# Sinkhorn attention and SwiGLU: a smaller mixing matrix, a reordered prologue, and two moved bursts

## The chip, the core and the metric

The program runs on one core of a Trainium2 chip. A core has engines that each run their own list of instructions in order and meet at semaphores: TensorE (PE in the profile; PEld is its weight load), VectorE (DVE), ScalarE (ACT), GpSimd (POOL) and SyncE (SP). TensorE multiplies a stationary operand (`lhsT`) by a moving one (`rhs`) into PSUM, of which this kernel uses eight banks of 512 floats a partition; VectorE and ScalarE read PSUM, and their copies out of it are called drains here. DMAs are issued from the queues of POOL, SP and ACT. The metric is the device time of one execution in microseconds, lower is better.

## The reference

Inputs are q, k, v of shape (4, 8, 768, 64), `sort_net` of shape (4, 8, 8, 8), and the weights of a SwiGLU block with a model width of 512 and an inner width of 1536. For each of 32 pairs of batch and head:

```python
P = sort_net
for _ in range(5):
    P = np.exp(P - np.max(P, axis=-1, keepdims=True))
    P = P / (np.sum(P, axis=-1, keepdims=True) + 1e-09)
    P = P / (np.sum(P, axis=-2, keepdims=True) + 1e-09)
k_sorted = np.einsum('bhij,bhjcd->bhicd', P, k_b)   # 8 blocks of 96 rows are mixed
v_sorted = np.einsum('bhij,bhjcd->bhicd', P, v_b)
attn = softmax(scale * q_b @ k_sb^T)                # within each block of 96
x = attn @ v_sb                                     # heads side by side: (3072, 512)
out = (silu(x @ w_gate) * (x @ w_val)) @ w_out
```

## The kernel before

**Sinkhorn (lines 218 to 241).** One 32x64 tile `p_ps` holds all matrices. Five rounds go back and forth between ScalarE (the exp) and VectorE (sums, reciprocals, products). The result is written to `p_bf`, repeated along a new axis of H = 8, in two operations of VectorE. TensorE has nothing to do yet: it runs small matmuls without use (`dots`, line 479) and 512-wide ones (`fill`, line 475), some of them tied to a round's `rowreds`.

**Mixing weights (lines 490 to 505).** `weights` transposes `p_bf` with the identity: eight matmuls for each half of the partitions write `w_ps`, where every one of 64 rows (head, block) holds the same matrix values that `mix_rows` on VectorE then masks to `rmix`, a block-diagonal matrix. With `rmix` as one operand a matmul mixes the blocks of k or v and transposes them at once.

**Chunks of batch 0 (lines 274 to 302, called in 506 to 517).** `q0_chunk`, `k0_chunk` and `v_chunk` each run some matmuls into a PSUM tile and drain it with VectorE ("v") or ScalarE ("s"). The last argument names the PSUM tile: "a" and "b" are two banks each, "x" is one, and "gen" rotates over three. A chunk has to wait until the tile's earlier reader is done. Queries come in two halves; `q0_chunk(0, 16, 8, "v", "a")` is the end of the first half.

**Attention units.** A unit is half of a batch's blocks for a pair of heads. `scores` runs its matmuls, `exps` the exps on ScalarE, `av` the value product on TensorE with a reciprocal and a product on VectorE (lines 362 to 366). The outcome is transposed into `xts`: on TensorE with a drain (`x_to`) for batch 0, and by a transposing DMA in SP's queue (`x_dma`) for the other batches. For batch 0's first four units the calls are written out by hand (lines 519 to 566); `early` starts the first gate and value tiles piece by piece, as the pieces of `xts[(0, 0)]` come.

**The feed-forward part.** It runs for eight half batches n: `gate(n, m)` and `value(n, m)` for twelve tiles m, each four matmuls of 384 columns, then `outp` for three output tiles of twelve matmuls. Gate tiles are read by a tanh on ScalarE, then by VectorE (line 420); value tiles by VectorE (line 433). All of them and some output tiles rotate through "gen".

**What sets the order.** On TensorE, ScalarE and POOL the order is that of the calls. `merge(main, side)` weaves the attention work of the next half batch into `ffn(n)`: each call of `ffn` has a cost (0.65 for a gate or value tile, 0.87 for a third of an output tile), and a side entry is called as soon as the sum of the costs has reached its time. `units` makes such entries: the scores of two units at `at`, the second unit's exp at `at + 1.3`, the two value products at `at + avs`. `v_pairs` makes entries for `v_pair_chunk`, the mixed values of batches 2 and 3, each with one drain of VectorE from "b" and one of ScalarE from "a"; `kqs` does the same for keys. VectorE's order is left to a scheduler after the prologue (line 569).

**Transfers.** POOL issues the loads in the order written. It copies batch 1's values (`copy_v`), then casts queries of batches 2 and 3 into a scratch (`q_cast`), then waits for batch 1's transposed output (`hold`, line 638) before it loads the next values. SP issues the transposing DMAs and the stores of the output.

Of the kernel before, what the change touches and what calls it, by code (L numbers as in the profile page):

```python
# [10 lines left out]
BF16 = mybir.dt.bfloat16  # L11
AF = mybir.ActivationFunctionType
ALU = mybir.AluOpType
# [4 lines left out]
def kernel(  # L18
# [191 lines left out]
    colred = const.tile([BH, 1, NB], FP32)  # L210
    p_bf = const.tile([BH, NB, H, NB], BF16)
    def pair_tile(name, tag):
        return psum.tile([128, 1024], FP32, name=name, tag=tag)

    def bank_tile(name, tag="gen"):
        return psum.tile([128, 512], FP32, name=name, tag=tag, bufs=3 if tag == "gen" else 1)

    p_ps = bank_tile("p_ps")[0:BH, 0:NB * NB].rearrange("p (i j) -> p i j", j=NB)
    for it in range(N_ITER):
# [15 lines left out]
        if it < N_ITER - 1:  # L235
            nc.vector.tensor_mul(p_ps, p_ps, colred.to_broadcast([BH, NB, NB]))
    for lo in (0, NB // 2):
        part = slice(lo, lo + NB // 2)
        nc.vector.tensor_tensor(
            p_bf[:, part], p_ps[:, part].unsqueeze(2).to_broadcast([BH, NB // 2, H, NB]),  # L240
            colred.unsqueeze(1).to_broadcast([BH, NB // 2, H, NB]), op=ALU.mult)
    copy_v(nc.scalar, 0, lowr, 4, 8)
    copy_v(nc.scalar, 0, lowr, 5, 8, 0, 40)

    def drain(eng, dst, src):
        if eng == "v":
            nc.vector.tensor_copy(dst, src)  # L247
        else:
            nc.scalar.copy(dst, src)  # L249
# [32 lines left out]

    def k0_chunk(at, n, eng, tag):
        dst = kqt_tile(0)[:, 0:GI * C].rearrange("p (n a c) -> p a n c", a=2, c=HC)
        rm = rmix[0].rearrange("p a (g two) i -> p two a g i", two=2)
        tp = chunk_tile("tk0", n // 8, tag).rearrange("p (l a n) -> p l a n", l=n, a=2)
        for lc in range(n):
            for two in range(2):
                nc.tensor.matmul(tp[two * D:(two + 1) * D, lc].rearrange("p a (g i) -> p a g i", g=H2),
                                 lhsT=k0[:, at + lc, :], rhs=rm[:, two], start=True, stop=True)  # L290
        drain(eng, dst[:, :, :, at:at + n], tp.rearrange("p l a n -> p a n l"))

# [25 lines left out]
    def scores(b, u, tag):  # L318
        half, g = divmod(u, H2)
        k_sb, k_at, q_sb, q_at = ((kqts[b], 0, kqts[b], GI * C) if b < 2 else  # L320
                                  (kqts["p"], (b - 2) * GI * C, kqts["q"], (b - 2) * GI * C))
        if tag == "gen":
            wide = None
            pss = [bank_tile("qk"), bank_tile("qk")]
        else:
            wide = pair_tile("qk", tag).rearrange("p (two n) -> p two n", two=2)
            pss = [wide[:, 0], wide[:, 1]]
        for i4 in range(4):
            at = (g * NB + half * 4 + i4) * C
            for two in range(2):  # L330
                lo = two * D
                nc.tensor.matmul(pss[two][:, i4 * C:(i4 + 1) * C],  # L332
                                 lhsT=k_sb[lo:lo + D, k_at + at:k_at + at + 128],
                                 rhs=q_sb[lo:lo + D, q_at + at:q_at + at + C],
                                 start=True, stop=True)
        return wide, pss
# [146 lines left out]

    dots(124)
    for it, n in ((1, 3), (2, 4), (3, 4), (4, 4)):
        nc.tensor.matmul(idle_ps[0:NB, 0:NB], lhsT=rowreds[it][:, :, 0], rhs=rowreds[it][:, :, 0],
                         start=True, stop=True)
        fill(idle_ps, n)

    w_ps = bank_tile("w_ps")[:, 0:NB * B * H].rearrange("p (i b h) -> p i b h", b=B, h=H)  # L490

    def weights(half):
        for i in range(NB):
            nc.tensor.matmul(w_ps[halves[half], i].rearrange("p b h -> p (b h)"),
                             lhsT=p_bf[:, i].rearrange("p a b -> p (a b)"),
                             rhs=ident[0:BH, 0:BH], start=True, stop=True)
# [4 lines left out]

    weights(0)
    weights(1)
    mix_rows(rmix[0][lowr, 0], lowr, 0)
# [7 lines left out]
    v_chunk(0, 56, 8, "s", "gen")  # L512
    k0_chunk(0, 16, "v", "a")
    k0_chunk(16, 16, "s", "b")
    k0_chunk(32, 8, "v", "gen")
    k0_chunk(40, 8, "s", "gen")
    q0_chunk(0, 16, 8, "v", "a")
    fill(idle_ps, 4)
    qk(0, 0, "a")
# [4 lines left out]
    qk(0, 2, "gen")  # L524
    idle_ps = bank_tile("idle_ps")
    fill(idle_ps, 2)
    av(0, 0, "a")
    fill(idle_ps, 2)
    av(0, 1, "b")
    fill(idle_ps, 1)  # L530
    xts[(0, 0)] = xtp.tile([128, H2, TW], BF16, name="xt0_0", tag="xt")
    qk(0, 3, "gen")
    av(0, 2, "a")
    x01 = xt_tile("x", 2)
    x_to(x01[:, 0], 0, 0)
    x_to(x01[:, 1], 0, 1)
    drain("s", xts[(0, 0)][:, 0:2, :], x01.rearrange("p g a b -> p g (a b)"))
    fill(idle_ps, 1)
    av(0, 3, "b")
    x2 = xt_tile("gen", 1)  # L540
    x_to(x2[:, 0], 0, 2)
    drain("s", xts[(0, 0)][:, 2:3, :], x2.rearrange("p g a b -> p g (a b)"))
    first = {}

    def early(n, kcs):
# [3 lines left out]
        for kc in kcs:  # L549
            nc.tensor.matmul(first[n], lhsT=sb[:, kc, ts(m, 128)], rhs=xts[(0, 0)][:, kc, :],  # L550
                             start=(kc == 0), stop=(kc == NKC - 1))

    early(0, (0, 1))
    early(1, (0, 1))
    x3 = xt_tile("x", 1)
    x_to(x3[:, 0], 0, 3)
    drain("v", xts[(0, 0)][:, 3:4, :], x3.rearrange("p g a b -> p g (a b)"))
    early(0, (2,))
    early(1, (2,))
    early(2, (0,))  # L560
    early(0, (3,))
    early(1, (3,))
    early(2, (1, 2, 3))
    gate_out(0, 0, first[0])
# [6 lines left out]

    def units(b, us, ats, avs=(1.9, 3.6), lag=3.1):
        us = list(us)
        todo = []
        for n, at in enumerate(ats):
            u, u2 = us[2 * n:2 * n + 2]
            held = []
            todo.append((at, lambda u=u, u2=u2, held=held: (qk(b, u, "b"), held.append(scores(b, u2, "a")))))
            todo.append((at + 1.3, lambda u2=u2, held=held: exps(b, u2, *held[0])))
            for w, tag, t in ((u, "b", avs[0]), (u2, "a", avs[1])):  # L580
                if b == 0:
                    todo.append((at + t, lambda w=w, tag=tag: av(b, w, tag)))
                    todo.append((at + t + lag, lambda w=w: drain("v", *xtr(b, w))))
                else:
                    todo.append((at + t, lambda w=w, tag=tag: (av(b, w, tag), x_dma(b, w))))
        return todo
# [44 lines left out]
    def q0_rest():  # L631
# [4 lines left out]
    merge(ffn(1), kqs(1, (0.6, 3.3, 7.1)) + vs(v_chunk, 16, (5.2, 5.8, 8.4, 9.1))  # L636
          + units(1, range(4), (11.0, 15.6), (1.3, 2.6)))
    hold = const.tile([1, 1], BF16)
# [3 lines left out]
    for s in range(4):  # L642
        copy_v(nc.gpsimd, 1, both, s)
    nc.vector.memset(kqt_tile("p")[:, 2 * GI * C:], 0.0)
    merge(ffn(2), units(1, range(4, 8), (0.0, 5.5)) + kqs("p", (13.0, 14.7, 20.7)) + v_pairs([(0, 22.5)])
          + [(13.0, lambda: q_dma(2)), (16.4, lambda: q_dma(3))])
    merge(ffn(3), v_pairs([(1, 0.0), (2, 5.1), (3, 6.9)]) + units(2, range(4), (9.8, 14.9)))
    merge(ffn(4), units(2, range(4, 8), (0.0, 8.0)))
# [38 lines left out]
```

## Time and profile before

| what | value |
|---|---|
| median of three runs | 246.46 us (246.25 to 246.61) |
| the profiled execution's own time | 246.0 us |
| its span | 244.2 us |
| TensorE matmuls busy | 237.1 us, 97% of the span, 2617 instructions |
| VectorE, ScalarE, POOL busy | 154.8, 112.3, 51.3 us |
| TensorE's granted clock, mean | 1.00 |
| batch 0's first scores start | 18.28 us |
| value tile (0, 1) starts | 25.27 us |

The page gives the busy time of each engine, the chain of work that ended last, and groups of instructions by line. A timeline row holds the start and the length of a group of equal instructions, its engine, line, operation, tiles (out<-in) and number; in brackets stands the idle time of the engine before it and what ended that. A matmul's length includes a tail in which the next one already runs: matmuls of 384 columns are 0.325 us long in the rows and 0.163 us apart. So a TensorE that looks busy can still have gaps, and starts are what counts. A wait shows as idle time with its releaser; a late transfer shows as a row whose releaser is a DMA.

### The profile page before, as it was taken

To read this page: it belongs to the slowest core of one execution; us is meant where nothing else is said; L and a number is where in the kernel's file an instruction comes from. 1 tells how busy PE (TensorE), PEld (TensorE's weight loads), DVE (VectorE), ACT (ScalarE), POOL (GpSimd) and SP (SyncE) were. 2 spreads that over 40 slices of the span, in tenths; PEclk is the share of its full clock that TensorE was granted. 3 is DMA by queue.
4 is the path that set the end of the run, shared out by engine and by line. 5 is a ranking of instruction groups with operands and counts; after the bars stand their busy time and mean duration, and the time that the engine had idled before them with its cause. 6 is when DMAs were issued, how large, how long until landed. Compare 5 with 4: busy or idle time off the path is not lost.

```text
span 244.2 us, 6162 instructions
## 1 busy us (share of the span) xinstructions
PE 237.1 (97%) x2617; PEld 139.4 (57%) x2617; DVE 154.8 (63%) x326; ACT 112.3 (46%) x189; POOL 51.3 (21%) x45
## 2 busy tenths in 40 slices
PE   7799999999999999999999999999999999999994
PEld 6375666676455565555555555565556555555543
DVE  6786789876664685777755845674675576445700
ACT  3977554467435435365543452254325334332312
POOL 5992139990002059200000000000000000000000
PEclk9999999999999999999999999999999999999999
DMA  5989999999996999410121212012111211110122
GB/s 99 215 129 208 206 213 213 204 214 190 161 137 139 190 162 159 119 43 3 46 75 32 62 59 71 8 59 63 32 43 46 75 36 43 43 43 3 43 86 86
DMA packets 39642, 24.77 MB, mean 101 GB/s; under 512 B 29376, under 2 KB 34368, under 8 KB 39616
## 3 DMA queue, kind: packets, MB, share of 16 engines
q0 software_dynamic: 19632, 14.16, 38.9%
q1 hardware_dynamic: 19840, 10.17, 17.0%
q8 instruction: 20, 0.33, 0.6%
q10 hardware_dynamic: 144, 0.07, 0.1%
q14 instruction: 6, 0.05, 0.1%
HBM read 28.32 MB, written 7.86 MB: 148 GB/s over the span
## 4 chain that ended last, share of the span: by engine, by line
PE 90%; DVE 4%; DMA 2%; ACT 1%; issue 1%; POOLq 0%
PE v_ps L428 25%; PE o_ps L445 25%; PE g_ps L410 25%; PE av_ps L359 3%; PE qk L332 3%; PE tkq L269 3%; DMA v<-in_v_dram 2%; PE o_ps L461 1%; PE idle_ps L477 1%; PE tv L300 1%; DVE st L365 1%; DVE vt L247 1%; PE tq L279 1%; PE tv L310 1%; PE g_ps L550 1%
## 5 line engine op out<-in xcount | busy, mean ns | idle before, releaser
L420 DVE SCALAR_TENSOR_TENSOR gs_sb<-th_sb,g_ps 128x384 bf16<-128x384 bf16 x96 | 52.9, 551 | 52.4 <-ACT th_sb L418 49.6
L428 PE MATMUL v_ps<-xt,wv_sb 128*128 128x384 bf16 x380 | 77.3, 326 | 0.0
L410 PE MATMUL g_ps<-xt,wg_sb 128*128 128x384 bf16 x376 | 76.6, 325 | 0.2
L418 ACT ACTIVATE th_sb<-g_ps 128x384 bf16<-128x384 f32 x96 | 47.1, 491 | 55.5 <-PE g_ps L410 52.7
L445 PE MATMUL o_ps<-wo,h 128*128 128x512 bf16 x276 | 64.2, 379 | 0.0
L433 DVE SCALAR_TENSOR_TENSOR h<-v_ps,gs_sb 128x384 bf16<-128x384 f32 x96 | 53.4, 556 | 7.6 <-PE tkq L269 0.5
L428 PEld LDWEIGHTS <-wv_sb 128*128 128x128 bf16 x380 | 35.3, 97 | 23.2 <-issue 0.2
L410 PEld LDWEIGHTS <-wg_sb 128*128 128x128 bf16 x376 | 34.9, 97 | 23.7 <-issue 0.4
L445 PEld LDWEIGHTS <-h 128*128 128x128 bf16 x276 | 26.1, 98 | 28.7
L450 ACT COPY o_sb<-o_ps 128x512 f32<-128x512 f32 x23 | 13.5, 586 | 49.0 <-PE o_ps L445 49.0
L148 POOL COPY vch<-v 64x1536 bf16<-64x1536 bf16 (+2 forms) x11 | 28.8, 2657 | 13.0 <-DMA v<-in_v_dram 12.9
L345 ACT ACTIVATE e_all<-qk 96x768 bf16<-96x768 f32 x30 | 23.3, 801 | 4.5 <-PE qk L332 4.5
L365 DVE TENSOR_TENSOR st<-av_ps,r_sb 96x512 bf16<-96x512 f32 x32 | 21.8, 680 | 0.3
L359 PEld LDWEIGHTS <-e_all 96*128 96x128 bf16 x256 | 11.8, 97 | 6.0 <-ACT e_all L345 1.7
L359 PE MATMUL av_ps<-vt,e_all 96*128 96x65 bf16 x256 | 13.1, 193 | 0.5 <-ACT e_all L345 0.5
L249 ACT CAST vt<-tv 96x1024 bf16<-96x1024 f32 (+1 forms) x11 | 10.1, 931 | 4.7 <-PE tv L310 3.6
L363 DVE RECIPROCAL r_sb<-av_ps 96x8 f32<-96x8 f32 x32 | 6.4, 199 | 8.7 <-PE av_ps L359 8.7
L247 DVE CAST vt<-tv 96x1024 bf16<-96x1024 f32 (+1 forms) x7 | 7.4, 1064 | 2.2 <-PE tv L310 1.7
L477 PE MATMUL idle_ps<-warm_sb 128*128 128x512 bf16 x25 | 7.6, 411 | 0.0
L247 DVE COPY oq_v<-o_ps 128x128 f32<-128x128 f32 x1 | 0.3, 292 | 9.3 <-PE o_ps L461 9.3
L395 POOL DMA_DIRECT2D q_scr<-in_q_dram x2 | 5.6, 3178 | 0.0
L146 ACT COPY vch<-v 64x768 bf16<-64x768 bf16 (+1 forms) x4 | 5.4, 1384 | 0.2 <-DMA v<-in_v_dram 0.2
(83 smaller groups left out, 129.8 us busy)
## 6 DMA issues: line engine op xcount, KB each, us to landing
out_dram<-o_sb SPq DMA_DIRECT2D x23, 256.0 KB, 2.0
v<-in_v_dram POOLq DMA_DIRECT2D x4, 384.0 KB, 12.6
wg_sb<-in_moe_w_gate_dram POOLq DMA_DIRECT2D x3, 512.0 KB, 11.2
wv_sb<-in_moe_w_val_dram POOLq DMA_DIRECT2D x3, 512.0 KB, 13.0
wo<-in_moe_w_out_dram POOLq DMA_DIRECT2D x3, 512.0 KB, 16.2
kqp<-in_k_dram POOLq DMA_DIRECT2D x2, 768.0 KB, 10.1
q_scr<-in_q_dram POOLq DMA_DIRECT2D x2, 768.0 KB, 18.8
v<-in_v_dram POOLq DMA_DIRECT2D x2, 768.0 KB, 9.8
```

Source lines behind the costliest of these rows:

```text
L148: eng.tensor_copy(dst, src.transpose([0, 2, 1]))
L247: nc.vector.tensor_copy(dst, src)
L345: nc.scalar.activation(e_all[:, n:n + 2, 0:4 * C], wide[0:C, :, 0:4 * C], AF.Exp, scale=scale)
L359: nc.tensor.matmul(o[:, two, i4, 0:D + 1], lhsT=e[:, i4 * C:i4 * C + 128], rhs=vt[:, 2 * g + two, half * 4 + i4, 0:D + 1], start=True, sto ...
L365: nc.vector.tensor_tensor(st.rearrange("p i two d -> p two i d"), o[0:C, :, :, 0:D], r_sb.to_broadcast([C, 2, 4, D]), op=ALU.mult)
L410: nc.tensor.matmul(g_ps, lhsT=wg_sb[:, kc, ts(m, 128)], rhs=xt[:, kc, :], start=(kc == 0), stop=(kc == NKC - 1))
L418: nc.scalar.activation(th_sb, g_ps, AF.Tanh, scale=0.5)
L420: nc.vector.scalar_tensor_tensor(gs_sb, th_sb, 1.0, g_ps, op0=ALU.add, op1=ALU.mult)
L428: nc.tensor.matmul(v_ps, lhsT=wv_sb[:, kc, ts(m, 128)], rhs=xt[:, kc, :], start=(kc == 0), stop=(kc == NKC - 1))
L433: nc.vector.scalar_tensor_tensor(h_tiles[n][:, m, :], v_ps, 0.5, gs_tiles.pop(m), op0=ALU.mult, op1=ALU.mult)
L445: nc.tensor.matmul(o_ps, lhsT=h_w[:, m, ts(t3, 128)], rhs=wo_sb[part][:, m % 4, :], start=(m == 0), stop=(m == NFC - 1))
L450: nc.scalar.copy(o_sb, o_ps)
```

## The change

These things are edited:

- `p_bf` is repeated 4 times instead of 8 and written by one operation; the mixing weights are then made by 32 matmuls of 32 rows each, four groups g for each block row i, instead of 16 of 64 rows.
- The useless matmuls are divided otherwise: 105 dots and 2 fillers instead of 124 dots at the start, one filler more in the last round, 3 fillers instead of 4 ahead of the first scores, one or two fewer between the first units.
- Batch 0's last query chunk runs ahead of the key chunks, in "x". The first key chunk is drained by ScalarE and the second by VectorE, the reverse of before. Of the two small key chunks ScalarE drains the first 16 of 32 columns each, and VectorE the rest.
- The fourth scores take one bank of "gen" and "x" ("mixed") instead of two of "gen"; the tile for the first two transposed pairs is in "gen" instead of "x" and drained in two copies.
- `early(0, (0, 1))` stands ahead of the third pair's transpose, and the pieces of the first three tiles follow in another order.
- `units` gets an argument `second`, which is 0.9 instead of 1.3 for batch 1's first four units.
- In `ffn(2)` the first value burst of batches 2 and 3 has the time 21.6 instead of 22.5, and the second is called there at 22.5 instead of at 0.0 in `ffn(3)`.

```diff
-    p_bf = const.tile([BH, NB, H, NB], BF16)
+    p_bf = const.tile([BH, NB, 4, NB], BF16)
...
-    for lo in (0, NB // 2):
-        part = slice(lo, lo + NB // 2)
-        nc.vector.tensor_tensor(
-            p_bf[:, part], p_ps[:, part].unsqueeze(2).to_broadcast([BH, NB // 2, H, NB]),
-            colred.unsqueeze(1).to_broadcast([BH, NB // 2, H, NB]), op=ALU.mult)
+    nc.vector.tensor_tensor(p_bf, p_ps.unsqueeze(2).to_broadcast([BH, NB, 4, NB]),
+                            colred.unsqueeze(1).to_broadcast([BH, NB, 4, NB]), op=ALU.mult)
...
-    def k0_chunk(at, n, eng, tag):
+    def k0_chunk(at, n, eng, tag, parts=None):
...
-        drain(eng, dst[:, :, :, at:at + n], tp.rearrange("p l a n -> p a n l"))
+        src = tp.rearrange("p l a n -> p a n l")
+        if parts is None:
+            drain(eng, dst[:, :, :, at:at + n], src)
+            return
+        drain(eng, dst[:, :, 0:parts, at:at + n], src[:, :, 0:parts])
+        return lambda e: drain(e, dst[:, :, parts:, at:at + n], src[:, :, parts:])
...
-        if tag == "gen":
+        if tag in ("gen", "mixed"):
             wide = None
-            pss = [bank_tile("qk"), bank_tile("qk")]
+            pss = [bank_tile("qk"), bank_tile("qk", "gen" if tag == "gen" else "x")]
...
-    dots(124)
-    for it, n in ((1, 3), (2, 4), (3, 4), (4, 4)):
+    dots(105)
+    fill(idle_ps, 2)
+    for it, n in ((1, 3), (2, 4), (3, 4), (4, 5)):
...
-    def weights(half):
-        for i in range(NB):
-            nc.tensor.matmul(w_ps[halves[half], i].rearrange("p b h -> p (b h)"),
+    for i in range(NB):
+        for g in range(4):
+            nc.tensor.matmul(w_ps[32 * g:32 * g + 32, i].rearrange("p b h -> p (b h)"),
                              lhsT=p_bf[:, i].rearrange("p a b -> p (a b)"),
                              rhs=ident[0:BH, 0:BH], start=True, stop=True)
...
-    k0_chunk(0, 16, "v", "a")
-    k0_chunk(16, 16, "s", "b")
-    k0_chunk(32, 8, "v", "gen")
-    k0_chunk(40, 8, "s", "gen")
-    q0_chunk(0, 16, 8, "v", "a")
-    fill(idle_ps, 4)
+    q0_chunk(0, 16, 8, "v", "x")
+    k0_chunk(0, 16, "s", "a")
+    k0_chunk(16, 16, "v", "b")
+    rest = [k0_chunk(at, 8, "s", "gen", 2 * NB) for at in (32, 40)]
+    for drain_rest in rest:
+        drain_rest("v")
+    idle_ps = bank_tile("idle_ps", "x")
+    fill(idle_ps, 3)
     qk(0, 0, "a")
     qk(0, 1, "b")
...
     qk(0, 2, "gen")
-    idle_ps = bank_tile("idle_ps")
-    fill(idle_ps, 2)
+    fill(idle_ps, 1)
     av(0, 0, "a")
     fill(idle_ps, 2)
     av(0, 1, "b")
-    fill(idle_ps, 1)
...
-    qk(0, 3, "gen")
+    qk(0, 3, "mixed")
     av(0, 2, "a")
-    x01 = xt_tile("x", 2)
+    x01 = xt_tile("gen", 2)
     x_to(x01[:, 0], 0, 0)
     x_to(x01[:, 1], 0, 1)
-    drain("s", xts[(0, 0)][:, 0:2, :], x01.rearrange("p g a b -> p g (a b)"))
-    fill(idle_ps, 1)
+    for g in range(2):
+        drain("s", xts[(0, 0)][:, g, :], x01[:, g].rearrange("p a b -> p (a b)"))
     av(0, 3, "b")
-    x2 = xt_tile("gen", 1)
-    x_to(x2[:, 0], 0, 2)
-    drain("s", xts[(0, 0)][:, 2:3, :], x2.rearrange("p g a b -> p g (a b)"))
...
+    x2 = xt_tile("gen", 1)
     early(0, (0, 1))
+    x_to(x2[:, 0], 0, 2)
+    drain("s", xts[(0, 0)][:, 2:3, :], x2.rearrange("p g a b -> p g (a b)"))
     early(1, (0, 1))
+    early(0, (2,))
     x3 = xt_tile("x", 1)
     x_to(x3[:, 0], 0, 3)
     drain("v", xts[(0, 0)][:, 3:4, :], x3.rearrange("p g a b -> p g (a b)"))
-    early(0, (2,))
     early(1, (2,))
-    early(2, (0,))
+    early(2, (0, 1, 2))
     early(0, (3,))
     early(1, (3,))
-    early(2, (1, 2, 3))
+    early(2, (3,))
...
-    def units(b, us, ats, avs=(1.9, 3.6), lag=3.1):
+    def units(b, us, ats, avs=(1.9, 3.6), lag=3.1, second=1.3):
...
-            todo.append((at + 1.3, lambda u2=u2, held=held: exps(b, u2, *held[0])))
+            todo.append((at + second, lambda u2=u2, held=held: exps(b, u2, *held[0])))
...
-          + units(1, range(4), (11.0, 15.6), (1.3, 2.6)))
+          + units(1, range(4), (11.0, 15.6), (1.3, 2.6), second=0.9))
...
-    merge(ffn(2), units(1, range(4, 8), (0.0, 5.5)) + kqs("p", (13.0, 14.7, 20.7)) + v_pairs([(0, 22.5)])
+    merge(ffn(2), units(1, range(4, 8), (0.0, 5.5)) + kqs("p", (13.0, 14.7, 20.7)) + v_pairs([(0, 21.6), (1, 22.5)])
           + [(13.0, lambda: q_dma(2)), (16.4, lambda: q_dma(3))])
-    merge(ffn(3), v_pairs([(1, 0.0), (2, 5.1), (3, 6.9)]) + units(2, range(4), (9.8, 14.9)))
+    merge(ffn(3), v_pairs([(2, 5.1), (3, 6.9)]) + units(2, range(4), (9.8, 14.9)))
```

More of the change, by code (lines that the diff above doesn't have):

```diff
@@ L500, in mix_rows @@
                                 w_ps[rows, :, b].transpose([0, 2, 1]), op=ALU.mult)
-    weights(0)
-    weights(1)
     mix_rows(rmix[0][lowr, 0], lowr, 0)
```

## The prediction

> **What bounds the kernel now.** I read the chain of waits first, then the timeline engine by engine for the stretches that the diff touches: the prologue up to 25.3 us, 60 to 65 us, 69 to 77 us and 100 to 109 us. All times are microseconds from the span's start.
>
> ```profile
> PE 90%; DVE 4%; DMA 2%; ACT 1%; issue 1%; POOLq 0%
> ```
>
> Nine tenths of the path are matmuls. From 25.27, where value tile (0,1) begins, TensorE works with small gaps to the end, so a delay or gain ahead of it shifts everything behind, unless a transfer holds TensorE later. The tenth that is not TensorE lies mostly in the prologue. TensorE, VectorE and ScalarE there:
>
> ```profile
> 11.19 0.76 PE L494 MATMUL w_ps<-ident,p_bf 32*64 32x32 bf16 x16
> 11.88 0.69 PE L279 MATMUL tq<-sel,qk 128*64 128x64 bf16 x32
> 12.51 2.27 PE L300 MATMUL tv<-rmix,vch 64*128 64x64 bf16 x64
> ...
> 18.28 0.39 PE L332 MATMUL qk<-kqt 64*128 64x96 bf16 x10
> ```
>
> ```profile
> 10.72 0.74 DVE L239 TENSOR_TENSOR p_bf<-p_ps,colred 32x256 bf16<-32x256 f32 x2
> ...
> 15.66 1.82 DVE L247 CAST kqt<-tk 128x1024 bf16<-128x1024 f32 x2 [0.19 <-PE tk L289]
> 17.42 0.69 DVE L247 CAST kqt<-tq 128x512 bf16<-128x512 f32 x1
> ```
>
> The first scores (18.28) follow the end of VectorE's third drain at 18.11. Further down, the transposed outputs are copied by ScalarE (22.18), and the first gate matmuls (23.03) start when the copy ends at 22.98:
>
> ```profile
> 22.18 1.36 ACT L249 COPY xt<-x_ps 128x768 bf16<-128x768 bf16 x2
> ```
>
> ```profile
> 22.68 0.34 PE L376 MATMUL x_ps<-ident,st 96*128 96x96 bf16 x4
> 23.03 0.48 PE L550 MATMUL g_ps<-xt,wg_sb 128*128 128x384 bf16 x2
> ```
>
> The second stretch: ScalarE copies an output tile between two exps, and TensorE, done with the gate at 63.11, waits for the second:
>
> ```profile
> 60.42 0.81 ACT L345 ACTIVATE e_all<-qk 96x768 bf16<-96x768 f32 x1 [1.05 <-PE qk L332]
> 62.42 0.59 ACT L450 COPY o_sb<-o_ps 128x512 f32<-128x512 f32 x1 [1.19 <-PE o_ps L445]
> 62.90 0.81 ACT L345 ACTIVATE e_all<-qk 96x768 bf16<-96x768 f32 x1
> ```
>
> ```profile
> 62.46 0.81 PE L410 MATMUL g_ps<-xt,wg_sb 128*128 128x384 bf16 x4
> 63.76 0.42 PE L359 MATMUL av_ps<-vt,e_all 96*128 96x65 bf16 x8 [0.49 <-ACT e_all L345]
> ```
>
> The third: an output store sits 1.68 us in SP's queue, and batch 1's fourth transposing DMA is issued behind it; it lands at 74.94, which POOL waits for:
>
> ```profile
> 70.87 1.68 SPq L452 DMA_DIRECT2D out_dram<-o_sb  x1
> 72.61 1.21 SPq L391 DMA_TRANSPOSE xt<-st  x1
> ```
>
> ```profile
> 74.99 0.18 POOL L639 COPY hold<-xt 1x1 bf16<-1x1 bf16 x1 [20.35 <-DMA xt<-st]
> ```
>
> Gate (2,0) starts at 74.83; its fourth matmul, at 75.32, reads that landing. That leaves 0.34 us. The last stretch, VectorE above TensorE:
>
> ```profile
> 101.56 1.22 DVE L247 CAST kqtp<-tkq 128x1024 bf16<-128x1024 f32 x1
> ```
>
> ```profile
> 101.61 1.90 PE L445 MATMUL o_ps<-wo,h 128*128 128x512 bf16 x8
> 103.44 0.64 PE L310 MATMUL tv<-rmixp,vch 64*128 64x64 bf16 x32
> ```
>
> **The matrix four-fold.** Now p_bf takes two operations of 0.41 and 0.40 us (10.72 to 11.47); new there is one of the same 32x256 form, done at 11.14. A fifth filler ends at 11.23, and a change of tile shape after a filler costs 0.10 (the last filler streams to 18.19, the scores start at 18.28): weights start at 11.33. They are 32 matmuls over four column groups instead of 16 over two. The end of the present row shows 31.5 ns between matmuls of one column group. Lower end: four groups side by side, eight rounds, 0.25 us. Upper end: no overlap, 32 x 31.5 ns = 1.0 us. In the tq row two column groups start 3 ns apart and 32 matmuls take 0.50 from first to last start, so a second group comes nearly free; I take 0.31, a round of four costing a quarter more. The last starts at 11.64 (now 11.78), and the queries and values behind it follow at the present distances: values at 12.38 instead of 12.51, -0.13 (-0.20 to +0.53). Their other waits are met: the first mask operation by 12.12, POOL's second copy at 11.93. The fewer dots and two added early fillers lie under the Sinkhorn chain.
>
> The row shows overlap between column groups. The Trainium skill, "TensorE: Matmul & The Clock Gate", section "What overlaps and what doesn't", says that a weight load overlaps a running matmul only where the row groups differ; here all four share one row group. By it and the same page's floor of about 25 ns per small matmul, the step would take an estimated 0.8 us and the sum below would be some 0.5 us worse; the tq row differs from it.
>
> **Queries ahead of keys, split drains.** Counted from the first value matmul, V: first scores now at V+5.77, behind VectorE's drains of 1.23, 0.68 and 0.69. After, the query chunk's matmuls (0.25) fall where TensorE now idles 0.30 before the keys, and its drain ends at V+3.58 on VectorE. The second key chunk starts, as now, when ScalarE frees its banks (V+3.14), so its VectorE drain runs V+3.87 to V+5.09. ScalarE does the first chunk (1.01, to V+4.48) and two half drains of 256 elements: 0.38 each from 0.59 for 512 and 1.01 for 1024 (0.30 to 0.59), done at V+5.04 (5.46 at worst). Scores start at V+5.14: -0.63 (-0.2 at worst). The two remaining halves (0.41 each on VectorE) and three mask operations (0.69) end 1.35 us after the first scores, ahead of the first reciprocal at 1.70; the third scores wait for them until 0.68, ahead of their exp at 1.78. Uncovered, they would cost 1.5.
>
> **Fourth scores, gates by head pairs.** Counted from the first scores, S. With the x bank instead of one that waits for an exp, the fourth scores move from 2.51 to 2.30 and their exps end at 3.56 instead of 3.91. VectorE's chain of reciprocals and products ends at 5.29 now and 5.14 then. Neither decides, for this does: the two pair copies of 0.48 start at 3.90 as now, because the first waits for both transposes. The first gate matmul starts at 4.43 (now 4.75), the second waits for the second copy until 4.81. The third pair's transpose, now at 4.40 (the 22.68 row), is queued on TensorE behind that, 4.97; its ScalarE copy moves from 4.78 to 5.35 and ends at 5.83, and the gate's third piece waits for it from 5.47 to 5.88. The fourth transpose follows (its 0.36 copy is covered by the 0.65 of matmuls behind it), then 1.14 of pieces: value (0,1) starts at S+7.35, now S+6.99. That is +0.36 (0 if the wait is shorter, +0.5). The tanh behind it is 0.69 later, VectorE 0.33 against TensorE; the next stop on it, unit 4's scores, has 0.14 left.
>
> **Exps moved.** The second exp starts right behind the first, 61.13 to 61.93, and the value product follows the gate at 63.11: -0.65. ScalarE's output copy still starts at 62.42, when its matmuls end; VectorE takes the second reciprocal first, and everything behind keeps its distances. At worst half returns.
>
> **The gate at 75 us.** By now TensorE is 0.40 + 0.65 = 1.05 early, the slack is 0.34, so up to 0.7 is lost if the landing stays at 74.94. What holds SP's store? One DMA engine spends 70.05 to 72.18 on a 16 KB packet of instructions, and its share of the third transposing DMA moves only then. TensorE's position sets when those instructions are fetched, so the packet should come early too. I take +0.10, near the lower end of 0 to +0.7. SP's and POOL's orders do not change; other transfers land 2 us or more ahead of their readers.
>
> **Value bursts moved.** The first burst would start at 102.58, behind one output part, but needs the banks of the 101.56 drain, done at 102.78: it waits 0.25 that output matmuls now cover. The second burst waits 0.17 for the first's drains. The stall of 0.30 ahead of the 108.46 gate shrinks to about 0.04, and that gate comes at 108.62: 0.25 + 0.17 + 0.04 - 0.30 = +0.16 (-0.1 to +0.3). POOL's value copies end at 99.3, ahead of both.
>
> **Sum.** -0.13 - 0.63 + 0.36 - 0.65 + 0.10 + 0.16 = -0.79. The profiled execution took 246.0 (span 244.2, 1.8 around it) and would take 245.2; it lies 0.46 under the median of the runs, 246.46, from which I forecast 245.67.
>
> **Rivals.** (B) The landing at 75 us stays: the gain there is cut to 0.34, then +0.16: 246.28. For it: POOL's copying of queries fills the DMA queues until 71.0 whatever TensorE does. Against: that packet. (C) The weight matmuls run one by one: +0.53 instead of -0.13; with less lost at 75 us, 246.2. For it: nothing in the trace has four column groups. (D) Slower: the clock drops. Between S+2.5 and S+5.9 a filler goes and waits come, so that matmuls stream some 1.7 of 3.4 us (now 2.5). If TensorE falls to the half rate that the fillers at 4.99 to 5.8 show (0.40 to 0.43 apart instead of 0.216), and takes as long to recover as from the first dot (1.20) to about 6.2, that costs half of 5 us, 2.5: 248.2. Against: 6.52 to 8.34 streams half the time, and the clock holds. It decides if that share falls under what holds there. The skill's "TensorE: Matmul & The Clock Gate" ("What's actually happening") lets the clock fall after an idle window of about 3.4 us; by it D does not happen, the longest gap here being 0.5.
>
> **How the numbers follow.** Forecast 0.58 (its own range 245.3 to 246.0), B 0.17, C 0.13, D 0.05; 0.07 for a stall not seen here, half of it slower. About 0.2%, 0.49 us, is what a measurement tells from no change. Faster is the forecast's case, 0.58; same takes B, C and part of the rest, 0.32; slower 0.10. The range 245.2 to 246.6 leaves out D and little more.
>
> **What would show it.** Values at 12.4 and scores at 17.5; a gap in TensorE ahead of the gate's third piece; value (0,1) at 24.9; no wait for an exp near 62.5; gate (2,0)'s fourth matmul near 74.4; new waits ahead of both value bursts near 102. I am wrong if four column groups don't overlap, if the landing holds at 74.9, or if matmuls of 384 columns after 22 us are more than 0.163 apart.

## The result, and the profile after

The changed kernel takes 245.27 us (median of 11 runs, 245.16 to 246.32) against 246.32 us for the kernel before (11 runs beside it, 246.05 to 246.88). The ratio is 0.9961, with a 95% interval of 0.9949 to 0.9973: faster by 0.4%. The forecast was 245.67 us.

The profiled execution of the changed kernel is the slowest of its eleven, 246.32 us with a span of 244.4. It is even 0.2 longer in span than the profiled execution of before (246.0, span 244.2). That alone asks for care: the two traces do not differ by the change's worth, so each step has to be read at its place. I did that with the 96 tanh operations of ScalarE, which both kernels run in the same order: the start of each in the one profile, less its start in the other, shows where time comes and goes. The difference is -0.31 us from the third tile on, -0.98 behind the exps near 62 us, 0.00 behind gate (2,0) near 75 us, and +0.18 from 109 us to the end. Outside the span lie 1.90 to 1.97 us in each run of the changed kernel, and 1.75 to 1.86 in the runs of the kernel before that stand beside the experiments.

The chain of work that ended last, on the page of the changed kernel, now runs through two transfers:

```profile
PE 86%; DMA 6%; DVE 4%; ACT 1%; POOL 1%; issue 1%; DVEq 0%; POOLq 0%
```

It had 2% of DMA before. By the page's next row, 4% of the 6% are the load of the keys in the prologue and 2% are the transposing DMA near 75 us; the shares are the lengths of these transfers, not what they cost. Now the four places. The columns of a timeline row are the start, the length (both in us), then engine, line, operation, tiles and number. First the weights, the first rows of TensorE's timeline from 11 us:

```profile
11.21 0.37 PE L497 MATMUL w_ps<-ident,p_bf 32*32 32x32 bf16 x32
...
12.14 1.04 PE L302 MATMUL tv<-rmix,vch 64*128 64x64 bf16 x30
```

Twice as many matmuls take 0.37 us where 16 took 0.76; values start at 12.14. Sinkhorn's result began 0.11 earlier in this execution (10.61 against 10.72), so 0.26 of the 0.37 is the step's. Next the keys, and the first tiles:

```profile
15.01 1.71 PE L286 MATMUL tk<-rmix,qk 128*64 128x64 bf16 x96 [0.22 <-DMA qk<-in_k_dram]
```

```profile
16.65 0.82 PE L479 MATMUL idle_ps<-warm_sb 128*128 128x512 bf16 x3
17.62 0.92 PE L334 MATMUL qk<-kqt 64*128 64x96 bf16 x24
...
22.05 0.70 PE L548 MATMUL g_ps<-xt,wg_sb 128*128 128x384 bf16 x2 [0.32 <-ACT xt L246]
22.59 0.33 PE L378 MATMUL x_ps<-ident,st 96*128 96x96 bf16 x4
22.81 0.50 PE L548 MATMUL v_ps<-xt,wv_sb 128*128 128x384 bf16 x2
23.49 0.32 PE L548 MATMUL g_ps<-xt,wg_sb 128*128 128x384 bf16 x1 [0.17 <-ACT xt L246]
...
24.96 0.81 PE L430 MATMUL v_ps<-xt,wv_sb 128*128 128x384 bf16 x4
```

The keys now wait for the transfer of their second half, which landed at 14.87: TensorE has come up against the load, in this execution. The first scores start at 17.62 instead of 18.28. The third pair's transpose (22.59) stands behind the second gate matmul, and the gate's third piece (23.49) waits for the copy of that pair. Value tile (0,1) starts at 24.96, 0.31 ahead of before, although the scores were 0.66 ahead.

The exps of the second stretch run back to back, and the wait of 0.49 ahead of the value product is gone; the product starts at 62.80 instead of 63.76:

```profile
60.11 1.50 ACT L347 ACTIVATE e_all<-qk 96x768 bf16<-96x768 f32 x2 [1.05 <-PE qk L334]
62.10 0.59 ACT L452 COPY o_sb<-o_ps 128x512 f32<-128x512 f32 x1 [0.49 <-PE o_ps L447]
```

```profile
62.15 0.81 PE L412 MATMUL g_ps<-xt,wg_sb 128*128 128x384 bf16 x4
62.80 0.41 PE L361 MATMUL av_ps<-vt,e_all 96*128 96x65 bf16 x8
```

At 75 us everything gained so far is given back in this execution. Gate (2,0) starts at 73.85 and stops ahead of its fourth matmul for batch 1's fourth transposing DMA:

```profile
73.85 0.87 PE L412 MATMUL g_ps<-xt,wg_sb 128*128 128x384 bf16 x3
75.33 0.32 PE L412 MATMUL g_ps<-xt,wg_sb 128*128 128x384 bf16 x1 [0.60 <-DMA xt<-st]
```

And the value bursts, with the small waits that the moved bursts bring:

```profile
101.61 1.04 PE L447 MATMUL o_ps<-wo,h 128*128 128x512 bf16 x4
102.83 0.64 PE L312 MATMUL tv<-rmixp,vch 64*128 64x64 bf16 x32 [0.18 <-DVE kqtp L244]
103.41 1.04 PE L447 MATMUL o_ps<-wo,h 128*128 128x512 bf16 x4
104.55 0.64 PE L312 MATMUL tv<-rmixp,vch 64*128 64x64 bf16 x32
...
108.64 0.81 PE L412 MATMUL g_ps<-xt,wg_sb 128*128 128x384 bf16 x4
```

The gate at 108.64 stood at 108.46 before: the bursts cost 0.17 to 0.18 in all.

### The profile page after: what moved, and what is told of

It is laid out like the page before. It is cut to its first block, busy times and chain, and to the rows that moved or that the text cites. A ratio compares the mean times of both kernels' runs of the same rounds, so it can differ in the third digit from the quotient of the medians.

```text
span 244.4 us, 6156 instructions
## 1 busy us (share of the span) xinstructions
PE 235.6 (96%) x2613; PEld 138.7 (57%) x2613; DVE 154.3 (63%) x326; ACT 112.3 (46%) x191; POOL 51.2 (21%) x45
## 4 chain that ended last, share of the span: by engine, by line
PE 86%; DMA 6%; DVE 4%; ACT 1%; POOL 1%; issue 1%; DVEq 0%; POOLq 0%
PE v_ps L430 25%; PE g_ps L412 25%; PE o_ps L447 23%; DMA qk<-in_k_dram 4%; PE av_ps L361 3%; PE qk L334 3%; PE tkq L266 2%; DMA xt<-st 2%; PE o_ps L463 1%; PE tv L312 1%; PE tv L302 1%; DVE gs_sb L422 1%; PE g_ps L548 1%; DVE st L367 1%; ACT xt L246 1%
## 5 line engine op out<-in xcount | busy, mean ns | idle before, releaser
L479 PE MATMUL idle_ps<-warm_sb 128*128 128x512 bf16 x24 | 6.6, 385 | 0.0
```

## The experiments

Two things were to be told apart: whether the steps add up as in the sum (theory S), and whether the landing near 75 us takes the gain away (theory L, the forecast's rival B). In the texts on record, S also stands for the time of the first scores. Medians of the kernel before in the three groups of runs were 246.37, 246.34 and 246.21 us.

**The third pair's transpose first.**

```diff
-    early(0, (0, 1))
     x_to(x2[:, 0], 0, 2)
     drain("s", xts[(0, 0)][:, 2:3, :], x2.rearrange("p g a b -> p g (a b)"))
+    early(0, (0, 1))
```

> The changed kernel with one thing else: the third pair's transpose and its copy stand ahead of the first two gate matmuls. Theory S (the +0.36 of the fourth step comes from that transpose being queued behind the second gate matmul): the copy of the third pair ends near S+5.3 instead of S+5.87 (S = first scores), no idle time of TensorE ahead of the gate's third piece, value tile (0,1) at S+6.9 instead of S+7.34; the time falls by 0.4 to 0.5 to about 244.8 us. Rival L (the fourth transposing DMA near 75 us lands when the query copies of POOL are done, whatever TensorE does): value tile (0,1) comes early all the same, but the wait of gate (2,0) near 75 us grows by as much and the time stays near 245.3. Rival N (the pair copies are late, not the transpose): value tile (0,1) stays within 0.1 of S+7.34 and the time near 245.3.

244.91 us, ratio 0.9947 (0.9931 to 0.9963). TensorE's timeline:

```profile
17.65 0.92 PE L334 MATMUL qk<-kqt 64*128 64x96 bf16 x24
...
22.00 0.34 PE L378 MATMUL x_ps<-ident,st 96*128 96x96 bf16 x4 [0.25 <-DVE st L367]
...
22.95 0.33 PE L548 MATMUL g_ps<-xt,wg_sb 128*128 128x384 bf16 x1
...
24.42 0.49 PE L430 MATMUL v_ps<-xt,wv_sb 128*128 128x384 bf16 x2
```

The wait ahead of the gate's third piece is gone and value tile (0,1) comes at S+6.77, where it was S+7.34. So the transpose was what was late, and the place of it costs 0.57, more than the whole step's 0.36. The rest of that step, by the difference to the S+6.99 of before, is worth 0.22. Of the 0.57 the time shows 0.36 by medians (the ranges, 244.78 to 245.72 here, overlap); at 75 us this profile loses 0.39.

**The value bursts as before.**

```diff
-    ... v_pairs([(0, 21.6), (1, 22.5)])
+    ... v_pairs([(0, 22.5)])
-    merge(ffn(3), v_pairs([(2, 5.1), (3, 6.9)]) + ...
+    merge(ffn(3), v_pairs([(1, 0.0), (2, 5.1), (3, 6.9)]) + ...
```

> The changed kernel with the value bursts as before (first at 22.5 in ffn(2), second at 0.0 in ffn(3)). Theory S (moving them costs 0.16): no waits of TensorE of 0.1 or more ahead of the two bursts near 102 to 105 us, the stall of 0.3 ahead of the gate near 108 is back, and the time falls by 0.1 to 0.2, to about 245.1 us. Rival G (moving them is a gain, since they fill the 0.3): 245.5 or more. Up to 100 us the trace is that of the changed kernel, so it also shows a second time how gate (2,0) near 75 us stands to the landing of the fourth transposing DMA: theory S has a wait of 0 to 0.3 there, rival L 0.7 or more.

245.16 us, ratio 0.9963 (0.9948 to 0.9978), 0.11 under the changed kernel by medians: too little for the times alone, but the trace shows where the 0.17 goes. No burst waits, and the stall of 0.3 is back (the matmuls of a tile are 0.163 apart, so a gate behind the tile at 107.18 could start at 107.83):

```profile
107.18 0.81 PE L430 MATMUL v_ps<-xt,wv_sb 128*128 128x384 bf16 x4
108.13 0.81 PE L412 MATMUL g_ps<-xt,wg_sb 128*128 128x384 bf16 x4
```

At 75 us this execution lost 0.58, between the two theories' figures.

**The second exp at 1.3 again.**

```diff
-          + units(1, range(4), (11.0, 15.6), (1.3, 2.6), second=0.9))
+          + units(1, range(4), (11.0, 15.6), (1.3, 2.6)))
```

> The changed kernel with 1.3 instead of 0.9 for the second exp of batch 1's first four units. Theory S (TensorE waited for an exp that ScalarE ran behind an output copy): the wait of about 0.5 ahead of the value product near 63.5 is back, everything from there to 75 us is 0.65 later, and the time is 245.9 us, 0.65 above the changed kernel. Rival L (gate (2,0) waits near 75 us for a landing that does not move): the 0.65 is slack there and the time stays within 0.2 of 245.3.

246.03 us, ratio 0.9989 (0.9978 to 1.0), 0.76 above the changed kernel. The wait is back, with the length it had:

```profile
62.07 0.81 PE L412 MATMUL g_ps<-xt,wg_sb 128*128 128x384 bf16 x4
63.37 0.42 PE L361 MATMUL av_ps<-vt,e_all 96*128 96x65 bf16 x8 [0.49 <-ACT e_all L347]
```

Theory S holds. The 0.65 is not slack: rival L would have left the time within 0.2.

**Batch 0's first tiles as before.** Fourth scores, copies, transposes and the order of the pieces as in the kernel before; queries, keys and the split drains as in the changed one.

```diff
-    fill(idle_ps, 1)
+    idle_ps = bank_tile("idle_ps")
+    fill(idle_ps, 2)
...
-    qk(0, 3, "mixed")
+    qk(0, 3, "gen")
...
-    x01 = xt_tile("gen", 2)
+    x01 = xt_tile("x", 2)
```

> The changed kernel with batch 0's units from the third scores to the first tiles as before: fourth scores in two banks of gen, one copy for two pairs, the third pair's transpose ahead of the first pieces. Theory S (this step costs 0.36): value tile (0,1) at S+6.99 instead of S+7.34, time about 244.9 us. Rival N (the step is neutral or a gain): value tile (0,1) at S+7.3 or later, time 245.3 or more. Rival L: value tile (0,1) early, but a longer wait near 75 us and 245.3.

245.29 us, ratio 0.9956 (0.9944 to 0.9968): as the changed kernel, a miss for theory S. The trace shows that it is not the clean undoing that I took it for:

```profile
18.88 0.59 PE L479 MATMUL idle_ps<-warm_sb 128*128 128x512 bf16 x2 [0.37 <-DVE rmixp L502]
19.31 0.41 PE L361 MATMUL av_ps<-vt,e_all 96*128 96x65 bf16 x8
```

The filler's tile is in "gen" again. By the row the filler waits 0.37 for the last mask operation (`rmixp`), which reads the tile of the weights, also in "gen"; VectorE runs the mask operations behind the late halves of the key drains. So the first value product starts at S+1.72 instead of S+1.25, and value tile (0,1) comes at S+7.45 instead of the S+6.99 of before. The bank of a matmul without any use is on the path. The two steps of the prologue are tied by it. The time is still that of the changed kernel because 1.80 us lie outside the span here, as before, and 1.95 in the changed kernel: the median span is 243.5 against 243.3.

**Batch 3's query copy later.** POOL issues it behind the value loads.

```diff
     q_cast(2)
-    q_cast(3)
...
     load_v(3, 0, 4)
+    q_cast(3)
```

> The changed kernel with the second query copy into the scratch (batch 3's) issued by POOL behind the loads of batches 2 and 3's values instead of ahead of batch 1's last transposed output. In the five profiles so far the fourth transposing DMA landed 1.1 to 1.3 us behind the end of that copy (2.0 in the kernel before), at 74.2 to 75.3 us, and gate (2,0) lost what TensorE was earlier than that. Theory L (that copy holds the landing): the DMA lands 2 to 3 us after its issue at 70.6, by 73.6, no wait of gate (2,0), everything from 66 to 100 us 0.8 to 1.0 ahead of the kernel before, and a time of 244.9 to 245.2. Theory K (the landing is held by something else, the instruction packet or the output store in SP's queue): landing at 74.2 or later, wait and time as in the changed kernel, 245.3. If the late copy holds up what follows it, batch 3's queries or the value copies, a new wait shows behind 90 us.

246.24 us, ratio 0.9998 (0.9987 to 1.0008). At 75 us theory L is right: the fourth transposing DMA landed at 73.22, 2.35 behind its issue, gate (2,0) did not wait, and TensorE stayed 0.86 ahead of the kernel before from 66 to 100 us. But nearly all of that was lost 30 us later: 0.18 to the moved bursts, as in the changed kernel, and the rest to a wait. The moved copy landed at 100.32; SP's queue waited for it with the transposing DMA of the queries, and the output that gate (3,0) needs stood behind, until 106.21 (SP's timeline; the first transpose is one output earlier):

```profile
91.78 1.21 SPq L393 DMA_TRANSPOSE xt<-st  x1
100.33 3.42 SPq L402 DMA_TRANSPOSE kqtq<-q_scr  x1
103.85 1.21 SPq L393 DMA_TRANSPOSE xt<-st  x1
```

**Only the exps moved, from the kernel before.**

```diff
-            todo.append((at + 1.3, lambda u2=u2, held=held: exps(b, u2, *held[0])))
+            todo.append((at + second, lambda u2=u2, held=held: exps(b, u2, *held[0])))
...
-          + units(1, range(4), (11.0, 15.6), (1.3, 2.6)))
+          + units(1, range(4), (11.0, 15.6), (1.3, 2.6), second=0.9))
```

> The kernel before with one thing else: 0.9 instead of 1.3 for the second exp of batch 1's first four units. Theory S: no wait for an exp near 63, TensorE 0.65 earlier from there to 75 us. Theory L: of this, what goes beyond the 0.4 of slack that gate (2,0) had over the landing at 74.94 is lost again near 75 us: the time falls by 0.4 to 0.65, to 245.7 to 246.0 us. Without a landing that holds it would be 245.7.

245.50 us, ratio 0.9968 (0.9957 to 0.9979), 0.84 under before by medians. In the trace the step is worth 0.66, of which 0.05 is lost at 75 us; the rest of the 0.84 lies in the kernel before, whose median execution is some 0.3 slower than its first profile. By medians this one number is most of what the whole change gains.

**Transpose first and bursts as before, together.** The two edits of the first and second experiment.

> The changed kernel with the third pair's transpose ahead of the first gate matmuls and the value bursts as before. Theory S adds the two: 0.36 + 0.11 below the changed kernel by medians, 244.8 us; value tile (0,1) at S+6.77. Theory L: the wait of gate (2,0) takes 0.4 of it in executions in which the second query copy ends at 73 us or later, as in the profiles so far.

244.74 us (244.46 to 245.0), ratio 0.9937 (0.9923 to 0.9951). All its runs lie below all of the changed kernel's: a version that beats both kernels. In its profile the copy ended at 72.18, and gate (2,0) ran through although TensorE was 1.65 ahead of the first profile of before; that lead lasted to the end.

**All three together**, with the later copy too.

> The three together: third pair's transpose first, value bursts as before, batch 3's query copy behind the value loads. Theories S and L: TensorE is 1.5 us ahead of the kernel before at 66 us and keeps it through 75 us: 244.4 to 244.6 us. Theory K: as without the moved copy, 244.8.

247.42 us (246.40 to 248.43), ratio 1.0041 (1.002 to 1.0061): slower. The wait seen with the later copy is now 2 us long (from 103.84, when the third matmul of the gate has run, to 105.82), and 0.9 us behind it the clock falls. In the second fence each row is a stretch; its busy times and numbers of instructions are those of PE, PEld, DVE, ACT and POOL, and then come the granted clock, the DMA share and the GB/s:

```profile
105.82 0.32 PE L412 MATMUL g_ps<-xt,wg_sb 128*128 128x384 bf16 x1 [1.82 <-DMA xt<-st]
...
107.86 1.48 PE L412 MATMUL g_ps<-xt,wg_sb 128*128 128x384 bf16 x4
```

```profile
104.00:106.00 2.00, 0.18 (x2) 0.00 (x0) 0.00 (x0) 0.14 (x1) 0.00 (x0) 1.00 0.90 215
106.00:108.00 2.00, 2.00 (x38) 1.21 (x38) 1.29 (x2) 1.50 (x2) 0.00 (x0) 0.68 0.59 224
108.00:110.00 2.00, 2.00 (x8) 0.89 (x7) 0.95 (x3) 0.49 (x1) 0.00 (x0) 0.50 0.00 0
110.00:112.00 2.00, 2.00 (x13) 1.18 (x12) 1.35 (x3) 0.49 (x1) 0.00 (x0) 0.96 0.00 0
```

The granted clock is 0.50 from 108 to 110, and by the means of the rows around it the half clock lasts some 3.4 us. Matmuls of 384 columns stand 0.32 apart from 106.9 to 110.1. The kernel's twelve times fall into two groups, six of 246.4 to 247.0 and six of 247.9 to 248.4; the mean granted clock is 0.993 in each of the upper six and 0.999 or 1.000 in the lower. The profiled one, 247.96, is of the upper group, and the gap of 1.6 us between the medians of the groups is what the half rate costs here (ten distances of 0.32 instead of 0.163). One execution with the bursts as before, 246.88, shows 0.993 too; without a trace of it, what came ahead is not known.

**Half of that copy later**: only its second four heads behind the value loads, with the two edits of the best version.

```diff
-    def q_cast(b):
+    def q_cast(b, lo=0, hi=H):
...
     q_cast(2)
-    q_cast(3)
+    q_cast(3, 0, H2)
...
     load_v(3, 0, 4)
+    q_cast(3, H2, H)
```

> The third pair's transpose first and the value bursts as before, and of batch 3's query copy only the second four heads behind the value loads of batches 2 and 3. With the whole copy there, the queue's query transposing DMA waited for it until 99.7 to 100.3 us and batch 1's last transposed output, behind it in SP's queue, landed at 105.8 to 106.2, which held gate (3,0). The whole copy took 14 us (86.3 to 100.3), so half of it should end near 93, the query transposing DMA land near 99 and the last transposed output by 100. Theory L: the first half ends near 69, the fourth transposing DMA lands near 72.5, gate (2,0) has 1 us of slack, nothing waits near 105, and the time is 0.0 to 0.2 below the 244.74 of the two edits alone: 244.5 to 244.7. If SP's queue is still held, gate (3,0) waits for a transposing DMA near 103 to 105 and the time is over 245.

244.99 us (244.65 to 245.24), ratio 0.9958 (0.9945 to 0.9972). The landings came as worked out (copies at 69.4 and 93.3, the fourth transposing DMA at 72.99, the last output at 100.05), nothing waits at 75 or 105 us, and the span of the profiled execution, 242.6, is that of the best version, 242.5. But the time misses the expected 244.5 to 244.7: it gives no gain on top. What makes its median 0.25 higher lies outside the span (2.3 against 1.9 us on the mean of the runs), and its cause is open.

**The weights one column group at a time.**

```diff
-    for i in range(NB):
-        for g in range(4):
+    for g in range(4):
+        for i in range(NB):
```

> The changed kernel with the two loops of the weight matmuls changed over: eight matmuls of one column group after the other, instead of four column groups in turn; the same 32 matmuls. Theory O (matmuls to different column groups run beside one another, those of one group come 25 to 31.5 ns apart, whichever way): 32 x 25 to 31.5 = 0.80 to 1.0 us from the first to the last start where the changed kernel took 0.20, values 0.6 to 0.8 later and a time of 245.9 to 246.1. Theory P (all 32 have one row group and one small operand, and their pace does not depend on the order): 0.20 us, 245.3. To 100 us this is otherwise the changed kernel, so gate (2,0) near 75 us and the landing ahead of it are seen once more, with TensorE later by the difference.

245.68 us, ratio 0.9982 (0.9973 to 0.9991), 0.41 above the changed kernel. Values start 1.88 behind `p_bf`, where they started 1.53 behind it.

```profile
11.27 0.72 PE L497 MATMUL w_ps<-ident,p_bf 32*32 32x32 bf16 x32
...
12.54 0.64 PE L302 MATMUL tv<-rmix,vch 64*128 64x64 bf16 x16
```

From the first to the last start it is 0.55 us, against 0.20 with the groups in turn. Theory O has the mechanism but not its size: matmuls of one group start 25 ns apart, yet each next group starts 0.12 behind the one before, while that one's last three are still to come. So a few matmuls of two groups run beside one another even here. Theory P is out: the order counts.

**The kernel before, once more.**

> The kernel before, unchanged, for a second profile: its first lay 0.3 to 0.4 us under the median of its runs. If the runs differ by when Sinkhorn's input lands, this shows as another start of p_bf and the same distances behind it; if by the landing near 75 us, as a wait of gate (2,0) there.

246.54 us. Up to 72 us every tanh starts 0.03 us later than in the first profile, as `p_bf` does; the difference is at 75 us, where the kernel before loses time as well. The landing came at 75.82, 0.9 later than in its first profile:

```profile
74.86 0.65 PE L410 MATMUL g_ps<-xt,wg_sb 128*128 128x384 bf16 x3
75.86 0.32 PE L410 MATMUL g_ps<-xt,wg_sb 128*128 128x384 bf16 x1 [0.35 <-DMA xt<-st]
```

## Why the forecast was right, and by how much it was off

Direction and range held; the time came out 0.40 under the forecast and 0.07 inside the lower end of the range. Of the 0.40, 0.14 is the kernel before, 246.32 beside the changed one instead of 246.46; the gain is 1.05 where I had 0.79. Step by step, in the profiles:

| step | forecast | measured | from |
|---|---|---|---|
| weights | -0.13 | -0.26 | p_bf to values 1.79 before, 1.53 in the changed kernel (1.53 to 1.71 in the eight others with its weights) |
| queries ahead, split drains | -0.63 | -0.53 | values to scores 5.77 before, 5.23 to 5.29 in nine others with this step; 5.48 in the changed kernel's profile |
| fourth scores, gates by pairs | +0.36 | +0.35 | S+6.99 to S+7.34 |
| exps moved | -0.65 | -0.67 | 0.66 with this step alone |
| value bursts | +0.16 | +0.17 | the tanh differences at 75 and 110 us |
| the gate at 75 us | +0.10 | 0.00 to 0.98 | by execution |
| outside the span | 0 | +0.15 | time less span: 1.80 before, 1.95 in the changed kernel |

**Weights.** Their 32 matmuls take 0.20 from first to last start, where I had 0.31: a round of four takes 25 ns, the four 3 to 4 ns apart, where I had 31.5 ns and a quarter. The gain of 0.26 lies beyond even my lower end of 0.20. The Trainium skill ("TensorE: Matmul & The Clock Gate", "The mechanism", at "What overlaps and what doesn't") lets a weight load overlap with matmuls in flight only when their row groups differ. The 32 here share one row group; one by one, at the 25 ns measured between starts in one column group, they would take an estimated 0.8 us, so in this trace the rule does not hold across column groups. Rival C is out.

**Queries and keys.** The drains end at V+5.09 as worked out (V the first value matmul). Missing is 0.10: the scores start 0.15 behind the end of the last drain they need (17.47 to 17.62 in the changed kernel, and 0.15 in nine of the ten profiles with this step), where my sum had 0.05. The fillers are not it: the last one had streamed by 17.30. No run undoes this step alone; its -0.53 is read at its place in the profiles. In the changed kernel's own profile the keys' second load added 0.24; no other execution shows more than 0.05.

**First tiles.** The wait that I named took the place that I gave it, to 0.01. The term is right, and the first experiment shows that it was there for the taking: 0.57 for one transpose's place. The experiment with the old first tiles shows what the forecast did not see, that this step also keeps a filler off a bank that comes free late behind the split drains. It shows a second thing: the time outside the span is 1.80 there and with the exps alone, and 1.92 to 1.95 in all versions with the new first tiles but the half copy (2.33). So 0.15 of cost goes with this step, a term that my sum did not have; its cause is open.

**Exps and bursts.** Right to 0.02, with the waits at the places named: for the bursts 0.25, 0.18 and 0.03 appear and 0.29 goes.

**The gate at 75 us** is where the working failed, in two ways. First the mechanism: I wrote that TensorE's position sets when the instruction packet comes and that it should come early with TensorE. It did not. In the profiles the packet starts at 68.5 to 72.1, and in the changed kernel, with TensorE 0.98 ahead, it came 2.0 later than before. In the changed kernel what holds the landing is what I had put under rival B, POOL's copying of queries. SP's queue there does not stand at the store, as it did before:

```profile
69.90 0.58 SPq L454 DMA_DIRECT2D out_dram<-o_sb  x1
70.52 1.22 SPq L393 DMA_TRANSPOSE xt<-st  x1
```

In the table "issue" is the start of the fourth transposing DMA in SP's queue, and "copy ends" is when the end of POOL's second query copy is signalled.

| kernel | issue | copy ends | packet | landing | lost at 75 us |
|---|---|---|---|---|---|
| changed | 70.52 | 73.99 | 72.07 to 73.04 | 75.29 | 0.98 |
| bursts back | 70.58 | 73.65 | 71.72 to 72.69 | 74.94 | 0.58 |
| exp back | 71.11 | 73.93 | 71.81 to 72.74 | 75.03 | 0.14 |
| first tiles back | 70.61 | 73.04 | 70.70 to 71.94 | 74.34 | 0 |
| transpose first | 69.99 | 72.94 | 70.46 to 71.34 | 74.16 | 0.39 |
| transpose first, bursts back | 69.84 | 72.18 | 70.26 to 71.23 | 73.48 | 0 |
| before | 72.61 | 72.94 | 70.05 to 72.18 | 74.94 | 0 |
| before, again | 73.52 | 73.40 | 69.78 to 72.43 | 75.82 | 0.51 |
| exps only | 72.38 | 73.06 | 69.98 to 71.96 | 74.76 | 0.05 |
| weights by group | 72.16 | 72.66 | 69.97 to 71.74 | 74.52 | 0.05 |
| copy later | 70.87 | 100.32 | 68.76 to 69.80 | 73.22 | 0 |
| all three | 70.52 | 99.65 | 68.51 to 69.43 | 72.86 | 0 |
| half the copy later | 70.61 | 69.41 (first half) | 68.56 to 70.19 | 72.98 | 0 |

In the first six rows the landing is 1.1 to 1.3 behind the copy, and 3.6 to 4.8 behind its own issue. In the last seven it is 2.30 to 2.38 behind its own issue: in three because the copy, or half of it, is out of the way, and in four because the DMA was issued late, at 72.2 to 73.5. In these four, the kernel before among them, the packet began between 69.8 and 70.1, and the entry ahead in SP's queue stood until 0.37 to 0.42 behind the packet's end. So I had read the kernel before rightly, but the changed kernel issues this DMA ahead of the packet and then meets the copy. That the copy holds the landing there is shown by the three runs that moved it. In these the packet came early too; but in the first six rows the landing keeps its distance to the copy within 0.2 us, and to the packet's end only within 0.6 (2.2 to 2.8). That the packet makes the issue late in the four rows is argued, since no run moves the packet alone.

Second, the offset. I added 0.46 to reach the median, as if every execution of before had it and the change would leave it. The second profile of before lost 0.51 at 75 us. For the changed kernel the opposite holds: its profiled execution, less the 0.98 that it lost, is 245.34, near its median of 245.27; with the bursts back 245.79 less 0.58 is 245.21 (median 245.16), with the exp back 246.15 less 0.14 is 246.01 (246.03). So the median execution of the changed kernel loses next to nothing at 75 us, while that of before loses some 0.3 (246.0 with none lost, medians of 246.2 to 246.4). Instead of +0.10 this stretch gave about -0.3 between the medians. This is read from own times and medians, since unprofiled executions have no trace; why the median landing is early enough for the one and not for the other stays open, the packet's place ahead of or behind this DMA's issue being the candidate. Rival B happened in full in the profiled execution (landing at 75.29, the gate's fourth matmul at 75.33 and not near 74.4, so one of the signs of being wrong came true), and not at the median. That the total lay in the range all the same is in part luck: the gain of some 0.4 more than forecast at this place and the 0.15 outside the span were both unforeseen, and of opposite sign. Rival D, the clock, did not happen: the mean granted clock was 0.998 to 1.000 in the changed kernel's runs.

## What to carry to other kernels

When one profile shows less than the times do, subtract the starts of an operation that both kernels run in the same order: each step then stands at its place, and what a single execution lost to a transfer does not hide the rest. Ahead of adding a constant between a profile and its median, take a second profile of the kernel before: the constant can be a wait that the change meets. A moved piece should be costed together with what now stands ahead of it in its queue: a transpose queued behind a gate matmul that waits for a copy cost 0.57, and a copy that frees one landing held another 30 us later in SP's queue.

## What the runs showed of the hardware

Small matmuls to the four column groups of one row group run beside one another when they come in turn (32 in 0.20 us), and only in part when they come group by group (0.55). The fourth transposing DMA landed 2.30 to 2.38 us behind its issue in seven executions, and 1.1 to 1.3 behind the end of POOL's copy in the six in which it was issued 2.3 us or more ahead of that end. And rival D's danger is real at another place: a TensorE wait of 2 us, from 103.8 to 105.8, was followed by 3.4 us of half clock in the profiled execution, and six of twelve executions have its mean granted clock of 0.993. The Trainium skill ("TensorE: Matmul & The Clock Gate", "What's actually happening") speaks of an idle window of about 3.4 us; here a wait of 2 us came ahead of the fall, and the half clock lasted as long as the page's busy window, about 3.4 us. That the wait is the cause is not shown by a run of its own. In the forecast I had set the page's figure against rival D; the changed kernel did not put it to the test, since TensorE's longest wait in the stretch named there was 0.32.
